# Score rests of a group of four heads issued behind the first pair's value products instead of behind the second pair's scores

## The chip, the cores and the metric
The kernel runs on one core of a Trainium2 chip. The metric is the device time of one execution in microseconds (us), the median of several runs. A core has a matrix engine (TensorE, PE in the profile; its weight loads are listed as PEld), a vector engine (DVE), a scalar engine (ACT), GpSimd (POOL), and a queue that issues transfers (SyncE, SP). Each engine takes its instructions in the order in which the program hands them over; semaphores order the engines against each other.

## The reference, cut to what matters
Three layers in float32. The change touches the first one only, attention with a sigmoid in place of a softmax:

```
q, k, v: (4, 12, 448, 64)                      # batch, heads, positions, width of a head
scores = q @ k^T / 8 - log(448)
attn   = sigmoid(scores)
x      = attn @ v     -> (1792, 768)           # tokens x (heads * width)
a, b   = x @ w_a, x @ w_b ;  g = a * b         # 768 -> 1536
x      = g @ w_out                             # 1536 -> 768
out    = soft mixture of 8 experts with 4 slots each (phi, w1, w2)
```

## The kernel before, in words
**Units of the attention.** The 48 heads are worked on as 24 pairs g = 0 to 23 (`NP = 6` pairs for each of the four batches). The keys of a pair are cut into chunks. For a chunk and a head the score matrix stands transposed, keys on partitions and the 448 queries along the free side, in one PSUM tile; the scalar engine reads it once, with the sigmoid, into an SBUF tile `a` (11 buffers), and `emit_PV` multiplies `a` with the values.

**Two ways of cutting 448 keys.** Up to pair 13, four chunks of 112. From pair `GQ = 14` on, three chunks of 128 keys, which leaves 64 keys of every head over: the *rests*. The rests of two neighbouring pairs (an even g and the odd g behind it, four heads, here called a group) are put together: `emit_S_rest(g)`, called for odd g, computes the 64 rest rows of pair g - 1 into partitions 0 to 63 and those of pair g into partitions 64 to 127 of one tile for each head of a pair, so that one sigmoid serves two heads' rests. The rest tiles are used by `emit_PV(g)` of the odd pair, behind its own three chunks (line 286), which completes both pairs' sums. There are five groups: (14, 15), (16, 17), (18, 19), (20, 21), (22, 23).

**PSUM tiles.** `ps_tile(tag, ...)` hands out the buffers of a tag in turn: four for `sc`, two for `ms`, two for `ab`. A buffer that is handed out again is written only after its last reader is done. `emit_S` takes two tiles for a chunk, one for each head:

```
by_ms = c == 0 and (g % 2 if g >= GQ else g >= GT0)
sc = [ms((n, S)) if by_ms and (g >= GQ or not h) else ps_tile("ab" if ab else "sc", [n, S], 2 if ab else 4)
      for h in range(2)]
```

So from pair 14 on chunk 0 of an odd pair stands in the two `ms` buffers, and every other chunk in two of the four `sc` buffers: the third chunk in a row that uses `sc` gets the buffers of the first again. `emit_S_rest` takes both its tiles from `ms()`. `emit_PV` uses `ab`.

**Order of issue.** `att()` is a generator that issues the attention piece by piece; each `yield` lets the surrounding loop (line 1136) put in one step of other work (operands of the next stage, on POOL and DVE, and transfers). Call S(g.c) the scores of chunk c of pair g (`emit_S`, matmuls of line 243, sigmoids of line 249), R(g) the rests (`emit_S_rest`, line 258), PV(g) the value products (`emit_PV`, lines 279 and 286), X(g) the copy of a finished pair out of PSUM (`emit_x`, line 309), and TK(g) the transposes and the splitting of k and q into two parts each (`emit_TK`, lines 191, 183, 184, 210, on DVE and ACT). In the stage of pairs 15 to 22 the matmuls run in this order (example for g = 17, then 18):

```
S(16.1) S(16.2) S(17.0) PV(16) | S(17.1) S(17.2) R(17) S(18.0) PV(17) | S(18.1) S(18.2) S(19.0) PV(18) ...
```

TK(g + 1) is issued to DVE at the start of step g, ahead of S(g.0). `kh`, `kl`, `qh`, `ql`, its results, have two buffers each, so TK(g + 1) waits for the scores of pair g - 1. In the last pair, g = 23, chunks 0 and 1 both stand ahead of PV(22), and S(23.2) and R(23) follow; the loop of line 1136 ends when a given sigmoid tile of pair 23 has been issued, and then the first products of the next stage (`unit`, line 843) are put ahead of PV(23).

**Transfers.** q, k and v are loaded three pairs ahead through SP. Two loads are issued inside `emit_S_rest`: q of pair 19 in R(15) and q of pair 23 in R(19), since they reuse a buffer that the rests still read.

**After the attention.** `unit` (line 843) multiplies batches 1 and 2 with w_a and w_b, `ab(3)` (line 660) does batch 3. At its seventh step (line 1181) SBUF is freed and the ring of slots opens into which w_out and the experts' weights w1 and w2 are loaded; the last stage consumes them as they arrive (lines 1229, 1249, 1275).

Of the kernel before, what the change touches and what calls it, by code (L numbers as in the profile page):

```python
# [20 lines left out]
C = 4  # L21
# [5 lines left out]
NP = H // 2  # L27
# [3 lines left out]
GQ = 2 * NP + 2  # L31
# [9 lines left out]
def body(ctx, tc, q, k, v, w_a, w_b, w_out, phi, w1, w2, out):  # L41
# [27 lines left out]
    def ms(shape=(128, S)):  # L69
        tags = banks[run["banks"]]  # L70
        tag = tags[run["ms"] % len(tags)]
        run["ms"] += 1
        return ps_tile(tag, list(shape), 4 if tag == "sc" else 2)
# [53 lines left out]
    def chunks_of(g):  # L127
        return (T, C) if g < GQ else (128, 3)
# [71 lines left out]
    def emit_TK(g):  # L200
        if g >= B * NP:
            return
        if g >= GT0:
            for nm in "kq":
                t = transposed(g, nm)
                split_heads(g, nm, t, dve.tensor_copy)
                if g >= GQ:
                    if nm == "k":
                        kr = atp.tile([128, 64], F32, tag="kr", name="kr", bufs=3)
                        act.copy(kr, t[:, 384:])  # L210
                        t = kr
                    whole[nm, g] = t
                if nm == "k" or g not in (GQ + 2, GQ + 6):
                    load_qkv(g + 3, nm)
            return
        tk = transposed(g, "k")
        if not g:
            tq = transposed(g, "q")
        split_heads(g, "k", tk, dve.tensor_copy)
        if not g:  # L220
            split_heads(g, "q", tq, act.copy)

    def emit_TQ(g):
        if g >= B * NP:
            return
        split_heads(g, "q", transposed(g, "q"), dve.tensor_copy)

    a_t = {}

    def emit_S(g, chunks):  # L230

        (kh, kl), (qh, ql) = stk[g]["k"], stk[g]["q"]
        n, _ = chunks_of(g)
        for c in chunks:
            ab = (g < NP or 2 * NP < g < GQ) and c == 2
# [3 lines that stand above are left out]
            cs = slice(c * n, (c + 1) * n) if g < GQ else slice(c, 384, 3)  # L239
            for i, (kx, qx) in enumerate(((kh, qh), (kl, qh), (kh, ql))):  # L240
                for h in range(2):
                    r = slice(64 * h, 64 * h + 64)
                    pe.matmul(sc[h], kx[r, cs], qx[r], start=(i == 0), stop=(i == 2))  # L243
            for h in range(2):
                sigmoid(g, h, c, sc[h], n)

    def sigmoid(g, h, c, sc, n):
        a = atp.tile([128, S], F32, tag="a", name="a", bufs=11)[:n]
        act.activation(a, sc, AF.Sigmoid, bias=nlog[:n], scale=1.0 / math.sqrt(D))  # L249
        a_t[g, h, c] = a  # L250

    def emit_S_rest(g):

        sc = [ms() for _ in range(2)]
        for d in range(2):
            for h in range(2):
                r, f = slice(64 * h, 64 * h + 64), 64 * d
                pe.matmul(sc[h][f:f + 64], whole["k", g - 1 + d][r], whole["q", g - 1 + d][r], start=True, stop=True)
        for h in range(2):
            sigmoid(g, h, 3, sc[h], 128)  # L260
        for d in range(2):
            del whole["k", g - 1 + d], whole["q", g - 1 + d]
        if g in (GQ + 1, GQ + 5):
            load_qkv(g + 4, "q")
# [3 lines left out]
    def emit_PV(g):  # L268
        if g < GQ:
            pv = pv_t[g] = ps_tile("sc", [128, S], 4) if g < 2 * NP else ms()  # L270
            for c in range(C):
                for h in range(2):
                    pe.matmul(pv[64 * h:64 * h + 64], qkv_t["v", g][:, h, c, :], a_t.pop((g, h, c)),  # L273
                              start=(c == 0), stop=(c == C - 1))
            return
        pv = pv_t[g] = ps_tile("ab", [128, S], 2)
        for c in range(3):
            for h in range(2):
                pe.matmul(pv[64 * h:64 * h + 64], qkv_t["v", g][:, h, c], a_t.pop((g, h, c)),  # L279
                          start=(c == 0), stop=False)  # L280
        if g % 2:
            a = [a_t.pop((g, h, 3)) for h in range(2)]
            for d in range(2):
                for h in range(2):
                    s = slice(64 * d, 64 * d + 64)
                    pe.matmul(pv_t[g - 1 + d][64 * h:64 * h + 64], qkv_t["v", g - 1 + d][s, h, 3], a[h][s],  # L286
                              start=False, stop=True)
# [15 lines left out]
    def emit_x(g):  # L303
        pv = pv_t.pop(g)
        qkv_t.pop(("v", g))
        b, kk = divmod(g, NP)
        if b:
            xt[g] = raw_x(b, kk)
            (dve.tensor_copy if g > GQ and g % 2 else act.copy)(xt[g], pv)
        else:  # L310
            xh = x0p.tile([128, S], F32R, tag=f"xh{kk}", name=f"xh{kk}")
            xl = x0p.tile([128, S], F32R, tag=f"xl{kk}", name=f"xl{kk}")
            act.activation(xh, pv, AF.Copy)
            dve.tensor_tensor(xl, pv, xh.bitcast(F32), op=ALU.subtract)
            xt[g] = (xh, xl)
        if g < GQ:
            load_qkv(g + 3, "v")
        if g >= GQ - 1 and g % 2:
            load_qkv(g + 4, "v")

    def att():

        emit_TK(0)
        yield 860
        for g in range(B * NP + 1):
            more = g < B * NP
            dense = g < NP or g >= 2 * NP
            first = ((0, 1) if g in (0, B * NP - 1) else (0,) if dense else ()) if more else ()
            if g:
                emit_TK(g + 1)  # L330
                if g > GQ and g % 2:
                    load_qkv(g + 3, "v")
                yield 430
            for c in first:
                emit_S(g, (c,))
                run["done"] = True
                yield 800
            if g:
                if g < NP and more:
                    emit_TQ(g + 1)  # L340
                    yield 430
                emit_PV(g - 1)
                if g <= GQ:
                    emit_x(g - 1)
                elif g % 2 == 0:
                    emit_x(g - 2)
                    emit_x(g - 1)
                yield 3200
            else:
                emit_TK(g + 1)  # L350
                yield 430
            if not more:
                return
            if not dense:
                emit_S(g, (0, 1))
                yield 1600
                emit_TQ(g + 1)
                yield 430
                emit_S(g, (2, 3))
                yield 1600  # L360
            else:
                if not g:
                    emit_TQ(g + 1)
                    yield 430
                for c in range(chunks_of(g)[1]):
                    if c not in first:
                        emit_S(g, (c,))
                        yield 800
                if g >= GQ and g % 2:
                    emit_S_rest(g)  # L370
                    yield 800

    PAIR = 860 + 4 * 800 + 3200
    att_g = att()
    att_state = [0]

# [193 lines left out]
    def fill_step():  # L570
        while fill:
            if next(fill[0], 0) is None:
                return
            fill.pop(0)
# [561 lines left out]
    for cost in att_g:  # L1136
        if then and then[0][0] in xt:
            then.pop(0)[1]()
        if not run.pop("trans", False):
            fill_step()  # L1140
        run.pop("done", None)
        if next(ops, 0) == 0:
            pu = pu or prep_u(0)
            next(pu, None)
        if (4 * NP - 1, 0, C - 1) in a_t:
            break
    run.pop("exp")()
    for _ in ops:
# [95 lines left out]
    for n in range(0, len(order1), 4):  # L1244
        _, g, x, _ = order1[n]
# [103 lines left out]
```

## Time and profile before

| | us |
|---|---|
| median of 3 runs (lowest to highest) | 664.09 (663.88 to 664.77) |
| the profiled execution's own time | 664.73 |
| its span, first to last instruction | 662.8 |
| PE busy in the span | 633.0 (96%) |
| ACT, DVE, POOL busy | 296.6, 380.1, 308.4 |

Times inside the profile count from the start of the span. In a timeline, consecutive instructions of one line and form are merged into a row: start, length of the whole, count, and in brackets the idle time ahead of it with what ended it. The chain of work that ended last is 83% PE. The stage that the change touches runs from 226 to 284 us.

### The profile page before, as it was taken

Reading aid. Unit: us, or ns where it says so; the run is one execution under the profiler, and the core shown is the slowest. Engines: PE = TensorE matmul, PEld = TensorE weight load, DVE = VectorE, ACT = ScalarE, POOL = GpSimd, SP = SyncE. Lnnn points to the kernel's source line nnn. Section 1 sums busy time; section 2 is a strip of 40 time slices with the busy share of each in tenths; the row PEclk is TensorE's granted clock in tenths of the full one; section 3 lists DMA queues with packets and bytes.
Section 4 is the critical chain, followed back from the end, with each engine's and each line's share of the span. In section 5 each row is a group of like instructions: output and inputs, shape, how many; then the busy total and the mean of one; then the engine's idle time right before and its main releaser. Section 6 shows DMA issues by size and latency. Waiting matters only on the chain.

```text
span 662.8 us, 10904 instructions
## 1 busy us (share of the span) xinstructions
PE 633.0 (96%) x4015; PEld 449.9 (68%) x4015; DVE 380.1 (57%) x557; ACT 296.6 (45%) x534; POOL 308.4 (47%) x236
## 2 busy tenths in 40 slices
PE   6999999999999999999999999999999998997685
PEld 4557777777776555489988989888879895442121
DVE  4765797788774879588777766744324322200013
ACT  4888889889774677754423322202010002110022
POOL 0233676777644248579976575543334441000000
PEclk9999999999999999999999999999999999998798
DMA  9998999989968676501213423242999999999998
GB/s 204 280 258 221 298 305 291 314 268 300 278 166 184 112 150 143 179 1 47 96 49 103 111 89 101 69 134 80 347 372 333 384 369 344 410 415 416 409 374 303
DMA packets 145396, 154.25 MB, mean 233 GB/s; under 512 B 74336, under 2 KB 121792, under 8 KB 142272
## 3 DMA queue, kind: packets, MB, share of 16 engines
q1 hardware_dynamic: 138768, 150.01, 72.5%
q10 hardware_dynamic: 6576, 3.56, 1.9%
q8 instruction: 32, 0.52, 0.3%
q14 instruction: 20, 0.16, 0.1%
HBM read 126.36 MB, written 27.17 MB: 232 GB/s over the span
## 4 chain that ended last, share of the span: by engine, by line
PE 83%; DMA 11%; ACT 2%; DVE 2%; issue 1%; ACTq 1%; SPq 0%; DVEq 0%
PE ab L660 28%; PE sc L843 16%; DMA e<-in_moe_w 9%; PE sc L243 8%; PE ab L843 8%; PE sc L273 5%; PE ab L279 3%; PE ms L195 2%; PE ms L936 2%; PE ms L581 1%; DMA gkp<-in_moe_w 1%; PE ms L480 1%; PE ms L493 1%; PE ab L243 1%; ACT a L249 1%; PE ab L286 1%
## 5 line engine op out<-in xcount | busy, mean ns | idle before, releaser
L454 POOL TENSOR_TENSOR w<-gk,cy 128x768 int32<-128x768 int32 x36 | 66.2, 1842 | 80.1 <-DVE gk L449 35.3
L249 ACT ACTIVATE a<-sc,sums 112x448 f32<-112x448 f32 (+1 forms) x147 | 83.1, 650 | 15.8 <-PE sc L243 15.7
L660 PE MATMUL ab<-t,wh 128*128 128x448 f32 x288 | 65.1, 371 | 0.0
L660 PEld LDWEIGHTS ab<-t,wh 128*128 128x128 f32 x288 | 53.4, 188 | 6.1 <-issue 1.3
L551 POOL TENSOR_TENSOR wl<-wr,wh 128x768 fp32r<-128x768 f32 x16 | 29.5, 1841 | 49.7 <-DVE wh L550 31.9
L551 POOL TENSOR_TENSOR wl<-w,wh 128x768 fp32r<-128x768 f32 x24 | 45.0, 1878 | 10.1 <-ACT wh L550 10.1
L667 ACT COPY misc<-ab 128x448 f32<-128x448 f32 x24 | 12.7, 531 | 82.1 <-PE ab L660 75.2
L1275 PE MATMUL ab<-e,gk 128*32 128x384 f32 x240 | 34.3, 560 | 9.5 <-DMA e<-in_moe_w 9.5
L670 DVE TENSOR_TENSOR misc<-misc,ab 128x448 f32<-128x448 f32 x24 | 14.8, 616 | 43.9 <-PE ab L660 43.9
L273 PE MATMUL sc<-a,vn 112*64 112x448 f32 x192 | 38.7, 545 | 0.2 <-ACT a L249 0.2
L243 PE MATMUL sc<-qh,kh 64*112 64x448 f32 (+1 forms) x147 | 34.9, 447 | 1.0 <-ACT qh L183 0.6
L723 ACT CAST wx<-T 128x384 fp32r<-128x384 f32 x21 | 10.8, 513 | 55.7 <-DVE T L745 39.1
L660 PE MATMUL ab<-xh,wh 128*128 128x448 f32 x144 | 34.9, 377 | 0.0
L660 PE MATMUL ab<-xl,wh 128*128 128x448 f32 x144 | 34.7, 376 | 0.0
L724 POOL TENSOR_TENSOR wx<-T,wx 128x384 fp32r<-128x384 f32 x23 | 24.6, 1070 | 21.1 <-ACT wx L723 18.0
L660 PE MATMUL ab<-xh,wl 128*128 128x448 f32 x144 | 34.3, 373 | 0.0
L660 PE MATMUL ab<-t,wl 128*128 128x448 f32 x144 | 34.3, 373 | 0.0
L724 POOL TENSOR_TENSOR wx<-wr,wx 128x384 fp32r<-128x384 f32 x29 | 32.4, 1117 | 3.7 <-ACT wx L723 3.6
L1322 DVE COPY o<-sc 128x384 f32<-128x384 f32 x10 | 5.4, 554 | 48.2 <-PE sc L1301 47.0
L447 DVE TENSOR_SCALAR mf<-gk 128x768 f32<-128x768 f32 x24 | 22.7, 947 | 17.2 <-ACT gk L430 17.2
L660 PEld LDWEIGHTS ab<-xl,wh 128*128 128x128 f32 x144 | 25.9, 188 | 9.4 <-issue 7.7
L1275 PEld LDWEIGHTS ab<-e,gk 128*32 128x32 f32 x240 | 9.8, 120 | 32.8 <-DMA e<-in_moe_w 20.7
(492 smaller groups left out, 1526.6 us busy)
## 6 DMA issues: line engine op xcount, KB each, us to landing
e<-in_moe_w SPq DMA_DIRECT2D x23, 1024.0 KB, 8.5
e<-in_moe_w SPq DMA_DIRECT2D x23, 768.0 KB, 15.1
wr<-ab SPq DMA_DIRECT2D x14, 768.0 KB, 4.4
ab<-w SPq DMA_DIRECT2D x24, 384.0 KB, 6.4
gk<-gk SPq DMA_DIRECT2D x24, 224.0 KB, 4.0
e<-in_moe_w SPq DMA_DIRECT2D x14, 384.0 KB, 8.8
wr_cv<-in_moe_w_a SPq DMA_DIRECT2D x6, 768.0 KB, 7.9
wr_all<-in_moe_w_b SPq DMA_DIRECT2D x6, 768.0 KB, 6.8
```

Source lines behind the costliest of these rows:

```text
L243: pe.matmul(sc[h], kx[r, cs], qx[r], start=(i == 0), stop=(i == 2))
L249: act.activation(a, sc, AF.Sigmoid, bias=nlog[:n], scale=1.0 / math.sqrt(D))
L273: pe.matmul(pv[64 * h:64 * h + 64], qkv_t["v", g][:, h, c, :], a_t.pop((g, h, c)), start=(c == 0), stop=(c == C - 1))
L279: pe.matmul(pv[64 * h:64 * h + 64], qkv_t["v", g][:, h, c], a_t.pop((g, h, c)), start=(c == 0), stop=False)
L447: dve.tensor_scalar(mf, m, LOW, HIGH, op0=ALU.max, op1=ALU.min)
L454: pool.tensor_tensor(thirds(w), m.bitcast(I32), thirds(cy_t.pop(x)), op=ALU.add)
L551: pool.tensor_tensor(wl, t, wh.bitcast(F32), op=ALU.subtract)
L660: pe.matmul(t, w[:, kk * 128:(kk + 1) * 128], xt[b * NP + kk][xi], start=(s == 0 and kk == 0), stop=(s == 2 and kk == KD - 1))
L670: dve.tensor_tensor(g, g, t, op=ALU.mult)
L724: pool.tensor_tensor(w[:, 1], t, w[:, 0].bitcast(F32), op=ALU.subtract)
L843: pe.matmul(t, w[:, wi, k * 128:(k + 1) * 128], xs[ORDER[m], k][xi], start=(s == 0 and k == 0), stop=(s == 2 and k == 2))
L1275: pe.matmul(sps[h][32 * j:32 * j + 32], hT[:, 2 * x + i, 2 * j + g], ring[order2[n + j]][0][:, i, c0:c0 + w], start=(g == 0 and x == 0 and ...
```

## The change
In `att()` the call of `emit_S_rest(g)` for odd g moves from behind the last score chunk of pair g to directly behind PV(g - 1). The number of yields of a step stays the same. The loop that ends with the last pair now looks for the tile of chunk 2 (`C - 2`) of pair 23, which is now issued last, in place of the rest tile (`C - 1`). No other line changes; the instructions are the same in kind and number.

```
--- before.py
+++ after.py
@@ -346,6 +346,9 @@
                     emit_x(g - 2)
                     emit_x(g - 1)
                 yield 3200
+                if more and g > GQ and g % 2:
+                    emit_S_rest(g)
+                    yield 800
             else:
                 emit_TK(g + 1)
                 yield 430
@@ -366,9 +369,6 @@
                     if c not in first:
                         emit_S(g, (c,))
                         yield 800
-                if g >= GQ and g % 2:
-                    emit_S_rest(g)
-                    yield 800
@@ -1142,7 +1142,7 @@
         if next(ops, 0) == 0:
             pu = pu or prep_u(0)
             next(pu, None)
-        if (4 * NP - 1, 0, C - 1) in a_t:
+        if (4 * NP - 1, 0, C - 2) in a_t:
             break
```

The matmuls of the example then run in this order:

```
S(16.1) S(16.2) S(17.0) PV(16) | R(17) S(17.1) S(17.2) S(18.0) PV(17) | S(18.1) S(18.2) S(19.0) PV(18) ...
```

and the sigmoids follow the same order on the scalar engine.

## Rows read from the trace of the kernel before

**Rows 1.** The page: span, and shares of the chain that ended last, by engine
```profile
span 662.8 us, 10904 instructions
...
PE 83%; DMA 11%; ACT 2%; DVE 2%; issue 1%; ACTq 1%; SPq 0%; DVEq 0%
```

**Rows 2.** Busy time by stage: length, engines, then granted clock, DMA share, GB/s
```profile
226.00:284.00 58.00, 57.52 (x381) 29.69 (x380) 43.31 (x64) 43.49 (x87) 29.67 (x25) 1.00 0.64 148
284.00:443.00 159.00, 159.00 (x870) 141.53 (x869) 118.92 (x165) 47.96 (x106) 115.65 (x103) 1.00 0.29 81
443.00:460.00 17.00, 17.00 (x104) 13.64 (x103) 7.47 (x13) 2.88 (x5) 4.20 (x3) 1.00 0.11 27
460.00:556.00 96.00, 95.02 (x635) 79.50 (x635) 32.05 (x64) 10.50 (x26) 36.78 (x20) 1.00 1.01 359
...
574.00:640.00 66.00, 54.22 (x396) 18.27 (x388) 2.08 (x3) 2.30 (x4) 0.00 (x0) 0.92 1.02 407
```

**Rows 3.** Waits of PE from 276 to 570 us, the longest of four
```profile
PE sc L925 <- ACT misc L905: 1.0, 1, 1.0
```

**Rows 4.** Timeline of PE, the step of pair 17: start, length, line, form
```profile
235.28 0.54 PE L243 MATMUL sc<-qh,kh 64*128 64x448 f32 x2
...
237.40 2.48 PE L279 MATMUL ab<-a,gk 128*64 128x448 f32 x12
239.80 0.54 PE L243 MATMUL sc<-qh,kh 64*128 64x448 f32 x2
...
241.29 0.98 PE L258 MATMUL ms<-gk,kr 64*64 64x448 f32 x8
242.21 0.54 PE L243 MATMUL sc<-qh,kh 64*128 64x448 f32 x2
...
243.08 2.48 PE L279 MATMUL ab<-a,gk 128*64 128x448 f32 x12
245.49 0.98 PE L286 MATMUL ab<-a,gk 64*64 64x448 f32 x8
```

**Rows 5.** Timeline of ACT in the same step (the last row, one sigmoid alone)
```profile
238.55 1.19 ACT L249 ACTIVATE a<-ms,sums 128x448 f32<-128x448 f32 x2
...
240.85 2.21 ACT L249 ACTIVATE a<-sc,sums 128x448 f32<-128x448 f32 x4 [1.11 <-PE sc L243]
...
242.41 0.64 ACT L249 ACTIVATE a<-sc,sums 128x448 f32<-128x448 f32 x1
```

**Rows 6.** Timeline of weight loads, the one that opens S(18.0)
```profile
242.21 0.25 PEld L243 LDWEIGHTS sc<-qh,kh 64*128 64x128 f32 x2 [0.70 <-ACT a L249]
```

**Rows 7.** Scores that waited in mid-chunk for a buffer: DVE, then PE
```profile
215.99 0.54 DVE ls_d L901
...
216.57 0.46 PE L243 MATMUL ab<-qh,kh 64*112 64x448 f32 x1 [0.17 <-DVE ls_d L901]
...
217.36 1.09 PE L624 MATMUL ms<-ident,misc 128*128 128x128 f32 x8
```

**Rows 8.** Timeline of PE, the step of pair 21
```profile
262.03 0.54 PE L243 MATMUL sc<-qh,kh 64*128 64x448 f32 x2
...
265.65 0.54 PE L243 MATMUL sc<-ql,kh 64*128 64x448 f32 x2 [0.48 <-DVE ql L184]
266.12 2.48 PE L279 MATMUL ab<-a,gk 128*64 128x448 f32 x12
```

**Rows 9.** Timeline of DVE: TK(20), end of TK(21), then what leads to ql(22)
```profile
248.04 0.58 DVE L183 CAST kh<-kn 128x448 fp32r<-128x448 f32 x1 [0.24 <-PE sc L243]
...
256.29 1.44 DVE L184 TENSOR_TENSOR ql<-gk,qh 128x448 fp32r<-128x448 f32 x1
258.77 0.39 DVE L751 CAST S2h<-s 128x448 fp32r<-128x448 f32 x1 [1.04 <-POOL s L771]
...
264.29 1.31 DVE L184 TENSOR_TENSOR ql<-qn,qh 128x448 fp32r<-128x448 f32 x1
```

**Rows 10.** Timeline of SP, the load of q of pair 23
```profile
258.30 2.10 SPq L153 DMA_DIRECT2D qn<-in_q  x4
```

More of the change, by code (lines that the diff above doesn't have):

```diff
@@ L348, in att @@
                 yield 3200
+                if more and g > GQ and g % 2:
+                    emit_S_rest(g)
+                    yield 800
             else:
@@ L368, in att @@
                         yield 800
-                if g >= GQ and g % 2:
-                    emit_S_rest(g)
-                    yield 800
     PAIR = 860 + 4 * 800 + 3200
@@ L1144, in body @@
             next(pu, None)
-        if (4 * NP - 1, 0, C - 1) in a_t:
+        if (4 * NP - 1, 0, C - 2) in a_t:
             break
```

## The prediction

> **What bounds the kernel now.** I read the page first, then the busy time by stage, the waits of PE, and the timelines of PE, ACT, DVE and SP in the one stage that the change touches. The chain that ended last is PE for 83% of the span, so a reordering of matmuls counts only by the gaps it closes or opens on PE [rows 1]. By stage, PE is busy 57.52 of 58.00 us in the stage of pairs 15 to 23, and 159.00 of 159.00 us from there to 443 us [rows 2]: whatever the attention gives or takes is handed on through products that run without a gap. The only waits of PE between 276 and 570 us belong to the short chain around the last softmax, four in all, the longest 1.0 us; their producers hang on PE itself, so they would not absorb a shift [rows 3]. Behind that stands a stretch limited by transfers: DMA share 0.11 until 460 us, then 1.01, and 1.02 at 407 GB/s up to 640 us with PE busy 54.22 of 66.00 us [rows 2]. The stream begins where `ab(3)` opens its slots at its seventh step, which is a place in PE's order, so the stream, and the end with it, moves by as much as PE does. A microsecond in the attention is therefore a microsecond at the end, either way.
>
> **The step, measured.** I take pair 17 as the model; the steps of 15, 19 and 21 have the same order. By start times [rows 4]: PV(16) from 237.40, S(17.1) at 239.80, R(17) at 241.29, S(18.0) at 242.21, PV(17) at 243.08. So S(17.1) with S(17.2) takes 1.49 us, R(17) 0.92 us, S(18.0) 0.87 us, together 3.28 us. The run of three chunks S(16.1) S(16.2) S(17.0) takes 237.40 - 235.28 = 2.12 us, against 1.49 + 0.87 = 2.36 us for three chunks that R parts: each time PE comes back to scores from another form it loses 0.24 us.
>
> **Part 1, what the change removes.** In the new order R(17) starts at 239.80, S(17.1) at 239.80 + 0.92 = 240.72, and the three chunks S(17.1) S(17.2) S(18.0) stand in one run. If nothing waited they would end at 240.72 + 2.12 = 242.84, 0.24 us ahead of 243.08. R behind PV isn't in the trace; the nearest row is PV's own rests behind PV's chunks, eight products of the same shape as R's, and they last the same 0.98 us [rows 4], so I leave R at 0.92. This is -0.24 us in each of four steps (15, 17, 19, 21). In step 23 the swap R(23) S(23.2) for S(23.2) R(23) leaves the number of returns to scores as it was: 0.
>
> The Trainium skill, TensorEngine Tiling (Array Packing), Tiling Modes, says that changing the tiling mode drains the engine; the trace agrees, with the 0.24 us, and by that rule alone the change would save 4 x 0.24 us, about 1 us. That is a rival below.
>
> **Part 2, what the change adds.** The same run of three chunks is the cost. All three take their two tiles from `sc`, which has four buffers: S(18.0) gets the buffers of S(17.1). In the old run S(16.1) S(16.2) S(17.0) the third chunk stood in `ms`, and in the old order S(17.1) S(17.2) R S(18.0) the 0.92 us of R lay in between, and the sigmoids of S(17.1) came first on ACT. That S(18.0) does hang on these sigmoids can be seen: its opening weight load is released by `ACT a`, just in time [rows 6].
>
> When will they be done? ACT is idle for 1.11 us ahead of 240.85, where it starts the first sigmoid behind PV(16), 1.05 us after PE began that chunk; four of them follow at about 0.52 us each, the last from 242.41 for 0.64 us, to 243.05 [rows 5]. In the new order the first two of these four places belong to R(17), and the third and fourth to S(17.1). R's matmuls last 0.98 us, so its first sigmoid starts at the same 240.85. Head 1 of S(17.1) is then read out at 243.05, where before it was done two places earlier, at about 242.0.
>
> S(18.0) reaches PE at 240.72 + 1.49 less the last chunk's change of form, about 242.13. Its first matmul is for head 0 (buffer free at 242.54), its second for head 1, which must wait until 243.05; everything behind it, and PV(17) above all, waits too. A release costs about 0.04 us (DVE done at 216.53, PE starts at 216.57 [rows 7]): 243.09. From there to the next product is 0.79 us in the one place where the trace shows scores that stopped at the second head for a buffer, 216.57 to 217.36 [rows 7]. The other restart within a chunk, two matmuls before PV, took 0.47 us [rows 8], and with two pairs of matmuls of about 0.2 us ahead of those two it gives 0.88. So PV(17) starts at 243.88 to 243.97 in place of 243.08: **+0.80 to +0.89 us, I take +0.83**. Bounds: if the restart costs nothing extra, the five matmuls left take 0.71 - 0.20 = 0.51 us, and the step loses 243.60 - 243.08 = +0.52; if there were no wait at all, -0.24; if the weight loads of both heads are held back too (0.25 us [rows 6]) +1.1.
>
> The Trainium skill, Perfetto Trace Analysis, Optimizing Tensor Performance, asks that independent matmul groups rotate through different PSUM banks so that the read-out of one overlaps the products of the next; that speaks against this change, and the trace gives it its size here [rows 5, 6].
>
> **The four steps do not add equally.** Steps 15, 17 and 19 have no gap before, so they lose 0.83 us each: 2.49 us. Step 21 already has one: S(21.1) starts at 262.03 and PV(21) at 266.12, 4.09 us where pair 17 took 3.28, since `ql` of pair 22 was late [rows 8]. The new order takes 3.28 + 0.83 = 4.11 us there, if `ql` is no longer the last: +0.02. It should not be. `ql` is done at 265.60, and what it hangs on runs over DVE and POOL back to TK(20), which waits for the scores of pair 18 [rows 9]; two lost steps stand ahead of that, so `ql` moves to 265.60 + 1.66 = 267.26. S(22.0) needs it at 262.03 + 2.49 + (243.09 - 239.80) + 0.41 = 268.22, behind its own wait. TK of the odd pairs waits for the scores that R now stands ahead of, 0.92 us later; TK(21) runs 1.66 + 0.92 us later, to 257.73 + 2.58 = 260.31, which is still before the POOL result that the next DVE instruction waits for, at 258.73 + 1.66 = 260.39 [rows 9].
>
> **What moves at no cost.** R now needs the two `ms` buffers of S(17.0) right behind PV(16). Their sigmoids end at 238.55 + 1.19 = 239.74, R starts at 239.80 [rows 4, 5]: 0.06 us less the release of 0.04. I cost it at 0, with 0 to +0.1 us for each of five steps as its bound. PV(17) needs the sigmoids of S(17.2) by its third chunk of keys, 1.6 us behind 243.9; they end at about 244.1. The loads of q of pairs 19 and 23 are issued earlier in the program, but between the same neighbours on SP; q of 23 goes out at 258.30 [rows 10], while R(19), a group before the step of 21, was over some 4 us earlier, so it is the queue's own pace that sets it: 0. POOL gets nothing moved. The sigmoids of R(23) come earlier and those of S(23.2) last; PV(23) reads them behind nine other products: 0. With stops of under a microsecond the granted clock stays at 1.00, as it does in the stage with the stop of step 21 [rows 2].
>
> **Sum.** 3 x 0.83 + 0.02 = +2.5 us. Against the profiled execution's own time, 664.73 us (span 662.8 and 1.9 around it), that is 667.2; its time is 0.64 us above the median of the runs, so on the scale of the medians 664.09 + 2.5 = **666.6 us**.
>
> **The rivals.**
> *A, the run of three chunks is free* (not slower). If S(18.0) got buffers that are long free, 0.24 us would be saved in each of steps 15 to 21, and the late `ql` would take back the part it isn't moved by: two savings reach TK(20), so only 0.48 of 0.96 us arrives: 663.6 us. If `ql` stopped being late as well, 0.96 + 0.81: 662.3. For it: PE's order really has one change of form less. Against: the buffer count, and what releases S(18.0) [rows 6].
> *B, the wait is there but smaller*: sigmoids of R start earlier, or head 0's three matmuls fill the time; +0.1 to +0.4 us per step, +0.3 to +1.2: 664.4 to 665.3. Against: matmuls alternate between the heads, so head 1 stops head 0 at the second one.
> *C, more is late*: R waits for `ms` by 0.1 us in five steps, and `ql` is late by another 0.8 us in step 21 since POOL and DVE now overlap otherwise: 2.5 + 0.5 + 0.8 = +3.8: 667.9.
> *D, the change does nothing*, since PE's order of matmuls within 3.28 us is only permuted: 664.1. That needs the buffers of A and no saving.
>
> **How the numbers follow.** Forecast 0.70, with its own range 665.6 to 667.5 (3 x 0.52 and 3 x 1.1, rounded). A and D 0.12 (of which 0.04 for more than the saving of 0.96, faster by over 0.2%), B 0.10, C 0.08. A difference of about 0.2%, 1.3 us, is what a measurement of this kernel can tell from none. Slower: forecast and C, 0.78; within 0.2%: B and the rest of A and D, 0.18; faster 0.04. The range 664.8 to 667.6 leaves out A and D, a third of B and half of C.
>
> **What would show it.** In the changed kernel's timeline of PE: the first three-chunk run from S(15.1) on has a gap ahead of S(16.0)'s second matmul, released by `ACT a L249`, and so for 18, 20 and 22, four waits of PE of some 0.5 to 0.9 us; R directly behind PV without a gap; PV(17) 4.1 us behind R(17)'s start; `ql` of 22 no longer a releaser. PE busy below 57.52 in the stage, and the stage's end some 2.5 us later, with the DMA stream as much later. I am wrong if the waits on `ACT a` are absent or the stage ends at the old time or earlier.

## The result, and the profile after

The changed kernel takes 668.03 us (median of 5 runs, 666.56 to 668.66) against 664.09 us before (5 runs, 662.88 to 665.77); ratio 1.0054, 95% interval 1.0033 to 1.0076, which is +3.6 us (2.2 to 5.0); the two medians alone are 3.9 us apart. It is slower, as forecast, but by more than the 2.5 us forecast and beyond the range's top of 667.6.

In the step of pair 17 the timeline of PE of the changed kernel now reads (start, length, line, form, and in brackets the idle time with what ended it):

```profile
239.66 1.15 PE L258 MATMUL ms<-gk,kr 64*64 64x448 f32 x8
240.74 0.54 PE L243 MATMUL sc<-qh,kh 64*128 64x448 f32 x2
...
242.54 1.06 PE L243 MATMUL sc<-qh,kh 64*128 64x448 f32 x2 [0.23 <-ACT a L249]
...
243.94 2.48 PE L279 MATMUL ab<-a,gk 128*64 128x448 f32 x12
```

From the first matmul behind PV(16) to PV(17) are 243.94 - 239.66 = 4.28 us, where before there were 3.28 [rows 4]. The gap stands where the prediction put it, in S(18.0), released by a sigmoid. The idle time in the bracket is only 0.23 us, less than the 0.5 to 0.9 us that the prediction named as its sign: the row of 1.06 us behind it is two matmuls of which the second waits too, as its weight load shows, so the loss is read from start to start, not from the bracket.

```profile
243.06 0.25 PEld L243 LDWEIGHTS sc<-qh,kh 64*128 64x128 f32 x1 [0.28 <-ACT a L249]
```

The waits of PE in the stage (226 to 290 us) are four, one for each of steps 15, 17, 19 and 21, and the wait on `ql` is gone:

```profile
PE sc L243 <- ACT a L249: 0.9, 4, 0.2
```

The timeline of ACT in the same step, to be held against [rows 5]:

```profile
240.80 1.16 ACT L249 ACTIVATE a<-ms,sums 128x448 f32<-128x448 f32 x2 [1.21 <-PE ms L258]
241.85 2.21 ACT L249 ACTIVATE a<-sc,sums 128x448 f32<-128x448 f32 x4
```

The first two sigmoids behind PV(16) are those of R(17); S(17.1) starts at 241.85 and its second head is read out at about 243.02 (0.52 us from one to the next, 0.65 for the last alone). S(18.0)'s second matmul needs that, and its weights are loaded at 243.06.

Step 21, where before [rows 8] `ql` was late, is the same 268.16 - 263.88 = 4.28 us:

```profile
263.88 1.15 PE L258 MATMUL ms<-gk,kr 64*64 64x448 f32 x8
...
268.16 2.48 PE L279 MATMUL ab<-a,gk 128*64 128x448 f32 x12
```

From PV(14) to PV(23) the stage takes 55.70 us (225.13 to 280.83) against 52.52 before (226.27 to 278.79): +3.18. From PV(23) to the first product of `ab(3)` both take 164.1 us. The profiled execution is 4.0 us longer in its span, because other things differ as well, two of them above all: it reached PV(14) 1.14 us earlier, and w_out's products (line 1229) took 5.74 us in place of 4.08. PE did not stand still for loaded tiles there; the granted clock was lower, as the repeat below shows.

### The profile page after: what moved, and what is told of

Same layout as the page of the kernel before. It is cut to its first block, busy times and chain, and to the rows that moved or that the text cites. A ratio compares the mean times of both kernels' runs of the same rounds, so it can differ in the third digit from the quotient of the medians.

```text
span 666.8 us, 10891 instructions
## 1 busy us (share of the span) xinstructions
PE 636.2 (95%) x4015; PEld 450.7 (68%) x4015; DVE 384.2 (58%) x557; ACT 296.6 (44%) x534; POOL 308.1 (46%) x236
## 4 chain that ended last, share of the span: by engine, by line
PE 83%; DMA 10%; ACT 3%; DVE 1%; issue 1%; ACTq 0%; SPq 0%; DVEq 0%
PE ab L660 28%; PE sc L843 16%; DMA e<-in_moe_w 8%; PE ab L843 7%; PE sc L243 7%; PE sc L273 5%; PE ab L279 4%; PE ms L195 2%; PE ms L936 2%; ACT a L249 1%; PE ms L581 1%; DMA gkp<-in_moe_w 1%; PE ms L480 1%; PE ms L493 1%; PE sc L1229 1%
## 5 line engine op out<-in xcount | busy, mean ns | idle before, releaser
L243 PE MATMUL sc<-qh,kh 64*112 64x448 f32 (+1 forms) x147 | 36.8, 444 | 1.9 <-ACT a L249 0.9
## 6 DMA issues: line engine op xcount, KB each, us to landing
ab<-w SPq DMA_DIRECT2D x24, 384.0 KB, 6.8
e<-in_moe_w SPq DMA_DIRECT2D x14, 384.0 KB, 8.8
```

## The experiments

All ratios are to the kernel before, run beside it on the same chip. "Stage" is PV(14) to PV(23), 52.5 us before and 55.7 after the change. A short diff is against the changed kernel, unless it says old order.

**Again.** No edit.

> The changed kernel once more, beside the others. Theory: the attention stage (PV(14) to PV(23)) costs 3.2 us more than before, three steps at +1.0 us and the step of pair 21 at +0.2, and the end moves by the same 3.2 us; what the first comparison shows beyond that (+3.9 in the medians) is scatter of the transfer-bound stretches: ratio 1.0048, total +2.5 to +3.9 us. Rival: the reordering costs a further 0.8 us behind the attention each time: +4 us again, with the stage at +3.2 and the stretch from PV(23) to the end at +0.8.

Measured: 667.3 us against 664.41, ratio 1.0052 (1.0035 to 1.0070), +2.3 to +4.6 us. Stage 55.74, so +3.2 again. From PV(23) to `ab(3)` 164.13 us, and from PV(23) to the end of the span 383.9 us, where before there were 384.0. Line 1229 takes 4.08 us, what it took before. Its products in the first changed run (the part at the lower clock), then all of them in this one (length, busy time of the engines, granted clock, DMA share, GB/s):

```profile
563.87:567.30 3.43, 3.43 (x20) 0.81 (x24) 0.16 (x1) 0.00 (x0) 0.00 (x0) 0.51 1.01 342
```

```profile
564.35:568.50 4.15, 4.08 (x48) 1.46 (x48) 0.91 (x2) 0.00 (x1) 0.00 (x0) 1.00 1.01 373
```

PE is busy throughout in both. In the first run the granted clock was 0.51 for these 3.43 us, the lower of its two levels (1.2 GHz), in this one 1.00; ahead of them PE had been busy for 1.90 of 2.87 us there and 2.38 of 3.30 us here, at 1.00 in both. So the 1.66 us are the clock of one execution and not a price of the new order. What lowered it that once, no run shows. The rival falls.

**Other buffers, same order.**

```
-            by_ms = c == 0 and (g % 2 if g >= GQ else g >= GT0)
+            by_ms = (c in (0, 2) and g % 2) if g >= GQ else (c == 0 and g >= GT0)
...
     def emit_S_rest(g):
...
-        sc = [ms() for _ in range(2)]
+        sc = [ps_tile("sc", [128, S], 4) for _ in range(2)]
```

> The new order of the matmuls, but the rests take their tiles from sc and chunk 2 of the odd pairs takes the two ms buffers, so that S(18.0) gets the buffers that R(17) had (read out first) and R(17) never waits for S(17.0). Theory (the buffers of S(17.1) are what the step waits for, and the ms buffers what stretches R): the step of pair 17 falls from 4.28 to 3.04 to 3.2 us, the waits of PE on the sigmoids are gone, and the total is 0.3 to 0.7 us below the kernel before (ql of pair 22 takes part of the four savings back): 663.4 to 663.8 where before is 664.1. Rival (the order itself is slow, because the sigmoids of the rests are served ahead of those that the next value products need): the step stays above 4 us, the total 3 us above before.

Measured: 663.97 us, ratio 0.9991 (0.9977 to 1.0005). Stage 52.40. The step of pair 17 on PE:

```profile
238.75 0.98 PE L258 MATMUL sc<-gk,kr 64*64 64x448 f32 x8
...
241.06 0.58 PE L243 MATMUL sc<-qh,kh 64*128 64x448 f32 x2
...
241.98 2.48 PE L279 MATMUL ab<-a,gk 128*64 128x448 f32 x12
```

3.23 us, just above the 3.04 to 3.2 expected, and the waits on sigmoids are gone. With the order of the change and other buffers the whole loss is gone: it is the buffers. The gain of one form change less (0.24 us) hardly shows, since S(18.0) still arrives just as R's second head is read out: its matmuls last 0.58 in place of 0.37 us.

**The old order on ACT alone.**

```
-        for h in range(2):
-            sigmoid(g, h, 3, sc[h], 128)
+        run["rest"] = lambda: [
+            sigmoid(g, h, 3, sc[h], 128) for h in range(2)]
...
                         emit_S(g, (c,))
+                        if c == 2 and "rest" in run:
+                            run.pop("rest")()
```

> The new order on PE, but the sigmoids of the rests are issued behind those of chunk 2, so that ACT serves S(17.1) first, as before the change. Rival (the order of the sigmoids on ACT is the cause): the step returns to about 3.3 us and the total to that of before. Theory (the cover that was lost is the 0.92 us of R on PE between S(17.1) and S(18.0); the sigmoids of S(17.1) can't begin until these scores are there, about 0.9 us later than R): S(17.1) is read out at about the same time as in the changed kernel (0.1 us earlier at most), the step takes 4.1 to 4.3 us, the total is 2.7 to 3.3 us above before.

Measured: 667.43 us, ratio 1.0044 (1.0029 to 1.0059). Stage 55.42, step 244.96 - 240.75 = 4.21 us. On ACT:

```profile
242.87 2.21 ACT L249 ACTIVATE a<-sc,sums 128x448 f32<-128x448 f32 x4 [2.19 <-PE sc L243]
```

ACT now stands idle for 2.19 us until S(17.1) is there, 2.12 us behind R's start, and reads its second head out 3.3 us behind it, as in the changed kernel (243.02 - 239.66 = 3.36). The order on ACT alone is not the cause: it is worth 0.07 us of a step. What is left is that PE has R no longer between the two chunks that share buffers; the next experiment puts it back there.

**Half the way.** The rests between chunks 1 and 2 of the odd pair.

```
-                if more and g > GQ and g % 2:
-                    emit_S_rest(g)
-                    yield 800
...
                 for c in range(chunks_of(g)[1]):
+                    if c == 2 and g > GQ and g % 2:
+                        emit_S_rest(g)
+                        yield 800
                     if c not in first:
                         emit_S(g, (c,))
```

> The rests moved only half as far: S(17.1) R(17) S(17.2) S(18.0). PE still has 0.92 us of R and a chunk between S(17.1) and S(18.0), ACT serves S(17.1) first; the number of returns to scores is that of before. Theory: no wait on a buffer of sc, the step takes 3.28 us as before, the total is within 0.3 us of before. Rival (any earlier place of the rests costs, since R comes closer to the sigmoids of S(17.0) or delays those of S(17.2) on ACT): the step grows by 0.5 us or more.

Measured: 663.9 us against 664.41, ratio 0.9987 (0.9973 to 1.0001), stage 52.46. The total is somewhat further below before than the 0.3 us expected, within the noise; the stage is within 0.1 us. The step is 243.67 - 240.39 = 3.28 us:

```profile
240.39 0.54 PE L243 MATMUL sc<-qh,kh 64*128 64x448 f32 x2
...
243.67 2.48 PE L279 MATMUL ab<-a,gk 128*64 128x448 f32 x12
```

The only wait of PE in the stage is the old one:

```profile
PE sc L243 <- DVE ql L184: 0.4, 1, 0.4
```

So an earlier place of R costs nothing in itself.

**The ms buffers free earlier.**

```
-            by_ms = c == 0 and (g % 2 if g >= GQ else g >= GT0)
+            by_ms = (c == 2 and g % 2 == 0) if g >= GQ else (c == 0 and g >= GT0)
```

> The changed kernel with the two ms buffers given to chunk 2 of the even pairs in place of chunk 0 of the odd ones: S(16.2) in ms, S(17.0) in sc. R(17) then writes over scores that ACT read one chunk earlier, and S(18.0) still needs the buffers of S(17.1). Theory (R is stretched from 0.92 to 1.08 us because its second head waits for the last sigmoid of S(17.0), a small separate term; the rest of the loss is the wait of S(18.0)): R takes 0.92 us again, the step of pair 17 takes 4.1 to 4.2 us in place of 4.28, the stage from PV(14) to PV(23) 55.1 to 55.4 us in place of 55.7, the total 2.6 to 2.9 us above before. Rival (R is longer for being behind value products, or what R writes over has no part in it): the step stays at 4.28, the stage at 55.7.

Measured: 667.09 us, ratio 1.0039 (1.0025 to 1.0053), stage 55.66. On PE:

```profile
240.44 0.98 PE L258 MATMUL ms<-gk,kr 64*64 64x448 f32 x8
...
243.32 1.06 PE L243 MATMUL sc<-qh,kh 64*128 64x448 f32 x2 [0.40 <-ACT a L249]
...
244.72 2.48 PE L279 MATMUL ab<-a,gk 128*64 128x448 f32 x12
```

Half my theory falls. R is short again (0.91 us to the next chunk at 241.35, so its stretch did come from the ms buffers), but the step stays at 4.28 us: S(18.0) goes on 243.32 - 240.44 = 2.88 us behind R's start, as it did in the changed kernel (242.54 - 239.66), and only waits 0.40 in place of 0.23 us. Here the delay ahead of the wait was swallowed by the wait. What sets the step in this run is ACT:

```profile
241.59 1.16 ACT L249 ACTIVATE a<-ms,sums 128x448 f32<-128x448 f32 x2 [1.21 <-PE ms L258]
```

R's sigmoids start 1.15 us behind R's start, stretched or not, and those of S(17.1) queue behind them. In the changed kernel two things hold S(17.1) back by nearly the same time, the sigmoids ahead of it on ACT and the stretched R ahead of it on PE, so that taking away either one alone (this experiment, and the one of the order on ACT) gives back 0 or 0.07 us. Both together were not run; by the rows of the two (0.91 us to S(17.1), 1.04 to its first sigmoid, 1.17 to the end of the second, 0.04 for the release, 0.88 to PV) I estimate a step of 4.04 us, so that about three quarters of the loss would stay.

**Twice the rests, old order.** Line 255 with `for d in (0, 1, 0, 1):` in place of `for d in range(2):`

> The old order, with the products of the rests issued twice (the second time over the first, so the values stay): about 0.7 us more of PE work in each of the five groups, without a wait. Theory (PE work in this stage is carried to the end one for one, except in step 21, where the late ql of pair 22 already leaves a gap of 0.8 us that takes it up): steps 15, 17 and 19 take 0.7 us more, step 21 0 to 0.2 more, the stage with step 23 about 2.9 us more, and the total 2.9 us above before. Rival (the stage has slack behind it, or the stretch of transfers adds to a delay): the total moves by under 2 or over 4 us.

Measured: 667.11 us, ratio 1.0040 (1.0025 to 1.0055): +1.7 to +3.7 us. Steps 15, 17 and 19 take 0.75 us more, step 23 0.74, and step 21, by the starts of PV(20) and PV(21), 6.44 us where it took 6.50: it takes up the whole addition. Stage 55.45, +2.93. What PE gains or loses here reaches line 1229 in full: its products start 282.85 us behind PV(23), as before (561.64 - 278.79). By the total alone, 1.7 to 3.7 us, a move just under 2 us, as the rival has it, is not excluded.

**The late ql, old order.**

```
-            for _ in range(3):
+            for _ in range(3 if i < 2 else 9):
                 yield
             split_x("S2", i, s2, cp, (f"S2h{i}", f"S2l{i}"))
```

> The old order, with the last rounding of the S2 operand issued six pieces later, behind TK(22), so that DVE does not stand still ahead of TK(22) for a result of POOL. Theory (ql of pair 22 is late because DVE waits 1.04 us for POOL, and this gap of 0.8 us is what hid the change's loss in step 21): step 21 takes 3.28 us from S(21.1) to PV(21) in place of 4.09, the wait of PE on ql is gone, the stage is 0.8 us shorter (51.7), the total 0.8 us below before, which is at the edge of what can be told. Rival (ql is late for the transposes or transfers of q): step 21 stays at 4.09.

Measured: 663.49 us, ratio 0.9984 (0.9970 to 0.9997), so 0.2 to 2.0 us below before; stage 51.72. Step 21:

```profile
261.85 0.54 PE L243 MATMUL sc<-qh,kh 64*128 64x448 f32 x2
...
265.13 2.48 PE L279 MATMUL ab<-a,gk 128*64 128x448 f32 x12
```

3.28 us, without a wait. The 0.8 us came from the rounding that stood ahead of TK(22) on DVE and waited there for POOL. With it behind, `ql` of pair 22 is done at 261.67 in place of 265.60, 3.9 us earlier: 1.04 us of that was the idle time, and DVE's instructions in TK(22) ran shorter in their new place as well (that of `kl` 0.63 us in place of 1.31), for a cause that was not looked into.

**The change in step 21 alone.** Old order, `emit_S_rest(21)` behind PV(20), the others as before.

> The change in step 21 alone, all other groups in the old order. Theory (the loss of 1.0 us and the old gap lie in the same place, and the longer counts): step 21 takes 4.28 us where it took 4.09, the stage 52.7 in place of 52.5, and PE's wait in S(22.0) is for the sigmoids, not for ql. Rival (the two add up): step 21 takes about 5.1 us.

Measured: one run, 664.57 us; stage 52.70. Step 21 takes 266.01 - 261.73 = 4.28 us, with PE's wait on a sigmoid:

```profile
264.61 1.06 PE L243 MATMUL sc<-qh,kh 64*128 64x448 f32 x2 [0.23 <-ACT a L249]
```

The longer of the two gaps counts, not their sum.

**The late ql mended in the changed kernel.** The edit of the seventh experiment in the new order.

> The changed kernel with the late rounding of S2 of the seventh experiment, which took 0.8 us off the old order. Theory (in the changed kernel ql of pair 22 is no longer what step 21 waits for, so there is nothing left to take off): step 21 stays at 4.28 us, the stage at 55.7, the total 3 us above before, as the changed kernel is. Rival (the two act apart): stage 54.9, total 2.2 us above before.

Measured: 666.72 us, ratio 1.0030 (1.0014 to 1.0045), stage 55.74, step 21 at 268.15 - 263.86 = 4.29 us. What took 0.8 us off the old order takes nothing off here. By the total alone (+0.9 to +3.0 us) the two theories wouldn't be told apart; by the stage they are.

**A version meant to beat both.** The other buffers of the second experiment, the late rounding of the seventh, and `emit_S_rest(g)` ahead of `emit_PV(g - 1)`.

> A version that should beat both kernels: the rests stand ahead of the value products, S(16.1) S(16.2) S(17.0) R(17) PV(16) S(17.1) S(17.2) S(18.0) PV(17), with the banks of the second experiment (rests in sc, chunk 2 of odd pairs in ms) and the late rounding of S2 from the seventh. The 2.4 us of PV(16) lie between R(17) and the chunk that writes over it, and PE comes back to scores once less per step. Theory (a chunk may follow the one that used its buffers only when ACT has had about 2.2 us behind the start of its sigmoids): S(18.0) no longer waits, R(17) waits 0.1 to 0.2 us for S(16.1), each of four steps gains 0.05 to 0.24 us, on top of the 0.8 us of the seventh experiment: total 1.0 to 1.8 us below before. Rival (the order with rests close behind other scores always costs): no better than the seventh experiment, or slower than before.

Measured: 663.75 us, ratio 0.9985 (0.9973 to 0.9997), no better than the seventh experiment. PE:

```profile
236.67 1.31 PE L258 MATMUL sc<-gk,kr 64*64 64x448 f32 x8
237.91 2.48 PE L279 MATMUL ab<-a,gk 128*64 128x448 f32 x12
```

S(18.0) is free of waits, the three chunks take 2.11 us (240.32 to 242.43), but R(17) takes 1.24 in place of 0.92 us, since it now follows S(16.1) by two chunks in the same buffers. The expected 0.1 to 0.2 us was 0.32, more than the form change gives back. The totals of this version and of the seventh experiment can't be told apart; the traces can, from PV(13), which stands ahead of all that moved, to PV(23): 57.98 us here, 57.35 in the seventh experiment, 58.14 before. The best that was run is the old order with the late rounding.

## Why the prediction was right in kind and too small

1. *What bounds the kernel*: right. PV(23) to `ab(3)` takes 164.1 us in every kernel. From PV(23) to the end of the span ten of the twelve profiled executions took 383.7 to 384.1 us, whatever the attention took.
2. *Part 1, 0.24 us for a return to scores*: right. With no wait in the way the three chunks take 2.11 us (last experiment) where 2.12 was read. In the changed kernel nothing of it is left, since S(18.0) only comes earlier to its wait. For step 23, 0 was right too (PV(22) to PV(23) 6.22 us before and after). The Trainium skill, TensorEngine Tiling (Array Packing), Tiling Modes, says that a change of the tiling mode drains the engine; the 0.24 us agree with that, but no row shows a drain as such.
3. *Part 2, the wait of S(18.0) for the buffers of S(17.1)*: right in place, order and releaser; the sum's term "**+0.80 to +0.89 us, I take +0.83**" was the step that failed. It measured 4.28 - 3.28 = 1.00. From the first matmul behind PV(16) to PV(17), 4.11 us was put together as 1.05 to the first sigmoid, 2.20 to the end of the fourth, 0.04 for the release and 0.82 from there to PV. Measured were 1.14 (R's sigmoids start later behind R than a score chunk's do), 2.22, 0.04 (243.02 to 243.06) and 243.94 - 243.06 = 0.88 us. The prediction called [rows 7] the one place where scores stopped at the second head for a buffer. That was a misreading. The trace of before holds a second, in the same form as S(18.0): S(23.1) comes back to the buffers of S(22.1), 2.02 us behind it, and its second weight load is released by a sigmoid 0.87 us ahead of PV(22):

```profile
271.70 0.25 PEld L243 LDWEIGHTS sc<-qh,kh 64*128 64x128 f32 x1 [0.19 <-ACT a L249]
...
272.57 2.48 PE L279 MATMUL ab<-a,vn 128*64 128x448 f32 x12
```

The list of PE's waits doesn't have it, since PE shows no idle time there. Read from it, the restart would have been right to 0.01 us.
4. *Step 21*: right that its old gap hides the loss, +0.19 where +0.02 was said, by the same 0.17. The experiments on step 21 (the late `ql` moved in either order, the change in this step alone) show the mechanism from three sides.
5. *What moves at no cost*: R was stretched by 0.16 us, beyond the bound of 0.1, and still cost nothing by itself, as the experiment with the `ms` buffers shows.
6. *The sum*: 3 x 1.00 + 0.19 = 3.2 us, which is the stage's +3.18 and +3.22, in place of 2.5. The totals agree: 3.6 (2.2 to 5.0) and 3.5 us (2.3 to 4.6).
7. *The range*: it was built from the bounds of the step around one median, and with 3.2 us for the change its middle would have been 667.3. The medians of the same changed kernel were 668.03 and 667.3, those of before 664.09 to 664.58. What differs between executions behind PV(23) had no place in the range: the first changed one took 386.0 us from there to the end, some 2 us longer than the ten, 1.66 us of that by the lower clock in line 1229, and the one with doubled rests 385.6, the difference all behind the start of line 1229. Only one of the five executions behind the 668.03 was profiled, so why their median lies 0.7 us above the repeat's stays open.

Rival A was run as the second experiment: removing the wait gives the time of before; of the 0.24 us that A expected in a step, 0.05 came. B falls, as the loss is 1.0 us a step, and D with it. C's 667.9 lies nearest to the first median, but by luck: R was stretched in four steps at no cost, and `ql` was not late again.

## What to carry to other kernels

When an instruction is moved, ask which two users of the same buffer it stood between: here a 0.92 us product between two chunks was the time in which ACT read the shared buffers out, and taking it away costs 1.0 us a step although the instructions are the same. In these steps a wait swallowed the delay ahead of it and the other wait in the same place, so terms in one step were joined by the longer one, not added. Read a loss from start to start of the next fixed point; the idle time named in the waits (0.23 us) was a quarter of it. And before a difference far behind the change is put down to scatter or to transfers, look at the granted clock there: it was the whole of the 1.66 us.

## What the runs showed that I had not expected

The first sigmoid behind eight quarter-array products of the rests starts 1.14 to 1.15 us after they begin, 0.1 us later than behind a score chunk of two halves (1.05), although the products last about as long (0.98 us). And a wait that ends about when its products are due did not show as idle time but as longer rows, since a row merges several products and the later ones start later: R 1.15 us in place of 0.98, S(18.0) in the second experiment 0.58 in place of 0.37.
